# One kernel, new order: every step's rank set anew, and the first MLP's last outputs sorted by inner halves

## The chip, the cores and the metric

The kernel runs on one core of a Trainium2 chip. The metric is the device time of one execution in microseconds (us). The engines are TensorE (PE; its weight loads are listed as PEld), VectorE (DVE), ScalarE (ACT), GpSimd (POOL) and SyncE (SP), which issues the DMAs.

## The reference

An attention with exponential features, then two MLPs of two dense layers each:

```python
proj = q @ w_phi; proj -= max|proj|; q_p = [exp(proj), exp(-proj)]     # the same for k
kv = sum_s k_p[s]^T v[s];  z = sum_s k_p[s]
attn = (q_p @ kv) / (q_p . z + 1e-6)          # 4 batches, 8 heads, 576 tokens, 64 columns
x = attn as 2304 tokens x 512
h = x @ w1_in (512 x 2048);  g = elu(h);                    x = g @ w1_out (2048 x 512)
h = x @ w2_in (512 x 2048);  g = h * clip(h + 3, 0, 6) / 6; out = g @ w2_out
```

The weights come as float64 words and are turned into float32 pairs on the chip.

## The kernel before

**Attention.** Eight units (`unit(u)`), each two heads of two batches. A unit projects keys and queries (`PJ`, PE, L319), takes the largest magnitude (`MX`, DVE, L329), subtracts it (`SB`, DVE, L343), exponentiates keys (`EX`, ACT, L352), adds up `KV` on PE (L381), copies the sums out (`ST`, ACT, L390), transposes the queries (`QT`, PE, L395 and L401), exponentiates them (`QE`, ACT, L408), multiplies (`NM`, PE, L431), divides (`RT`, `RB`, DVE), transposes back (`XT`, PE, L453) and writes a piece of x (`XC`, ACT, L457).

**MLPs.** x has four token blocks of 512 and one of 256 (number 4), and four column chunks `d` of 128, of which chunks 0 and 1 are the one half of the inner dimension, 2 and 3 the other; in each half, the chunk is named by `kk` (chunks 0 and 2 are `kk` 0, chunks 1 and 3 are `kk` 1). Blocks 0 and 1 form pair 0, blocks 2 and 3 form pair 1. For each pair the first product is done by seven products (Winograd's form of Strassen's scheme, `P1` to `P7`, L711) instead of eight, block 4 directly (`H`, L725). Each operand is kept as a high and a low float32r part, and a product is three matmuls per piece. The operands are prepared by `prepare(m, pr)`: for each `kk` four sums or differences of x pieces (DVE, L688; called S1 to S4) and seven operands, each with a high part copied by ACT (L694) and a low part found by DVE or POOL (L697). x is overwritten in place. The hidden results pass through joins (DVE, L738), the activation (ACT, L745 to L748), the gate (DVE, L752), and a split into high (ACT, L756) and low (DVE, L759) in buffers `ga` (blocks 0 and 2) and `gb` (blocks 1, 3 and 4), two of each. The second product (`O`, PE, L776) makes four outputs (`d` 0 to 3) for each block, in the ring `y` of three PSUM banks; each output is added into x by DVE (`sums`, L788). That goes on for `NP` = 8 groups `g` of 256 hidden columns in each MLP: g 0 to 7 are the first, 8 to 15 the second. Weight conversion goes over ACT, DVE and POOL (L627 to L678).

**Order.** PE's order in the MLPs is written out by hand in the list `order`: products, outputs of this group and outputs left from the group before. In the last group of the first MLP (g = 7) the outputs of blocks 0 and 1 stand between the products of pair 1, those of blocks 2 and 3 at the end; the two halves of block 4's outputs (`kept`) come after the first two products of g = 8. The second MLP's operands can only be prepared when the outputs that complete x are added.

Every other engine's order is made by a planner, `in_order`, before the program is written out: it simulates all steps with assumed durations and, on each engine, takes among the steps that could start within `WINDOW` (0.3 us) of the soonest the one with the lowest rank. The engines then run these fixed orders, each waiting for its own data. The planner holds DVE steps marked `port` and POOL steps apart from each other. The ranks are times: in attention the unit's number times `PERIOD`, less the length of what follows, plus an offset for the kind of step; for operands the time at which PE is due to need them less `PREP` (16 us for the first MLP, 22 us for the second); for sums of outputs and for gates the time at which their product is due to end.

```python
s.rank = u * PERIOD - tail[id(s)] + BIAS.get(s.kind, 0.0)     # attention
rank = need[m, pr, op] - PREP[m]                              # operand's high and low part
when = clock + us                                             # sums and gates
if d == KD - 1:          # the last MLP-1 output of a block: its pair's prepare(1, ...) is listed
```

Of the kernel before, what the change touches and what calls it, by code (L numbers as in the profile page):

```python
# [24 lines left out]
PERIOD, PROJ, TURN = 21.5, 0.22, 0.19  # L25
BIAS = {
# [3 lines left out]
}  # L30
# [3 lines left out]
PREP = (16.0, 22.0)  # L34

# [8 lines left out]
class Step:  # L44
    def __init__(self, engine, us, fn, after=(), rank=0.0, takes=(), uses=(), port=False, behind=(), rows=128):
        self.engine, self.us, self.fn, self.rank, self.port, self.rows = engine, us, fn, rank, port, rows
        self.after, self.behind, self.takes = list(after), list(behind), list(takes)
        for t in uses:
            t.users.append(self)
        self.start = self.end = None  # L50


LATENCY = {"PE": 0.25, "DVE": 0.11, "ACT": 0.14, "POOL": 0.12, "SP": 2.2, "NONE": 0.0}
WINDOW = 0.3


def in_order(steps, rings):
# [13 lines left out]
    def soonest(s):  # L71
        t = max([0.0] + [x.end + LATENCY[x.engine] for x in s.after] + [x.start for x in s.behind])
        extra = {}
        for k in s.takes:
            had = taken[k.ring]
            at = len(had) + extra.get(k.ring, 0) - rings[k.ring]
            extra[k.ring] = extra.get(k.ring, 0) + 1
            if at < 0:
                continue
            if at >= len(had):  # L80
                return None
            for x in had[at].users:
                if x.end is None:
                    return None
                t = max(t, x.end + LATENCY[x.engine])
        return t

    known = {}
    while len(out) < len(steps):
# [23 lines left out]
        if s.port or s.engine == "POOL":  # L113
            port = s.end
# [34 lines left out]
def attention_then_two_mlps(  # L149
# [107 lines left out]
    def unit(u):  # L257
# [247 lines left out]
        add("ST", "ACT", 0.75, stat, after=[f"KV{j}{h}" for j in ("k0", "k1", "x8") for h in range(2)],  # L505
# [29 lines left out]
        for s in reversed(mine):  # L535
            tail[id(s)] = s.us + tail.get(id(s), 0.0)
            for x in s.after:
                tail[id(x)] = max(tail.get(id(x), 0.0), tail[id(s)] + LATENCY[x.engine])
        for s in mine:
            s.rank = u * PERIOD - tail[id(s)] + BIAS.get(s.kind, 0.0)  # L540
# [269 lines left out]

    def on(engine, us, fn, rank, after):
# [3 lines left out]
    def split(m, pr, op, kk, at, deps, e_hi, e_lo):  # L815
# [3 lines left out]
        hi = on(e_hi, (0.05 + 0.55 * size, 0.1 + 0.56 * size), bind_(x_hi, e_hi, pr, op, kk, at), rank, deps + home)  # L819
        lo = on(e_lo, (0.1 + 0.6 * size, 0.1 + 1.3 * size), bind_(x_lo, e_lo, pr, op, kk, at), rank, [hi])  # L820
# [4 lines left out]
    def prepare(m, pr):  # L825
        b0, b1 = 2 * pr, 2 * pr + 1
        POOL = nc.gpsimd
        for kk in range(2):
# [3 lines left out]
            def add(op, out_, in0, in1, alu, deps):  # L832
                e = POOL if soon else V
                s = on(e, (0.7, 1.4), bind_(x_add, e, out_, in0, in1, alu), need[m, pr, op] - PREP[m] - 1, deps)
# [4 lines left out]
            def cut(op, at, deps, e):  # L839
                here = soon and op in EARLY  # L840
                return split(m, pr, op, kk, at, deps, POOL if here else nc.scalar, POOL if here else e)

            r11 = cut("A11", a11, final[a11], V)
            r12 = cut("A12", a12, final[a12], POOL)
            r22 = cut("A22", a22, final[a22], V)
# [4 lines left out]
            cut("S2", a11, [s2], V)  # L850
            cut("S3", a21, [s3], POOL)
            cut("S1", a22, [s1], V)
            cut("S4", a12, [s4], POOL)
# [7 lines left out]
    for g in range(2 * NP):  # L861
# [63 lines left out]
    for g in range(2 * NP):  # L925
        m, w = g // NP, 2 * (g % NP)
        lead = first[g] - W_IN_LEAD
# [28 lines left out]
        lead = first_o[g] - W_OUT_LEAD  # L956
# [10 lines left out]
    def finish(m, g, b, fi, after, ps_, ring, when):  # L967
        key = (g, b, fi)
        if ring:
# [31 lines left out]
    for x in order:  # L1001
# [53 lines left out]
        else:  # L1055
# [6 lines left out]
            when = clock + us  # L1062
# [90 lines left out]
```

## Time and profile before

| | us |
|---|---|
| median of 3 runs | 938.45 (938.14 to 939.03) |
| the profiled execution: its time | 938.99 |
| the profiled execution: its span | 937.2 |
| PE busy | 903.2 (96%) |
| DVE, ACT, POOL busy | 677.9, 567.3, 398.0 |

The span runs from the first to the last instruction in the trace; the time is 1.8 us longer. Busy times are sums over stages that differ: PE is nearly always busy in the MLPs and less so in attention and between the stages.

### The profile page before, as it was taken

What the parts mean: (1) busy time and instruction counts of PE and PEld (TensorE: products, weight loads), DVE (VectorE), ACT (ScalarE), POOL (GpSimd) and SP (SyncE); (2) the same over time, 40 slices, a digit from 0 to 9 for tenths busy, and PEclk for the clock granted to TensorE, in tenths of its full rate; (3) what the DMA queues carried; (4) which work ended last, traced back from release to release, by engine and by line L of the source; (5) the groups of instructions that cost most, each with busy time, mean ns of one, the idle gap of its engine ahead of it and who ended that gap; (6) DMA issues with size and microseconds to landing.
All of it is one profiled execution on the core that took longest, in us unless ns stands there. A gap on an engine that the chain in (4) does not pass through costs nothing.

```text
span 937.2 us, 17621 instructions
## 1 busy us (share of the span) xinstructions
PE 903.2 (96%) x6792; PEld 759.3 (81%) x6792; DVE 677.9 (72%) x1202; ACT 567.3 (61%) x1207; POOL 398.0 (42%) x570
## 2 busy tenths in 40 slices
PE   8999999899999999999999978999999999999998
PEld 7888888778888888888888856888888888888886
DVE  6888887854868686868677789577777676767565
ACT  5687676877656565656566646765555554545331
POOL 0238721353535353535352555655544444444200
PEclk9999999999999999999999999999999999999999
DMA  7534420001111111111111000121111111110013
GB/s 223 158 114 119 134 82 2 1 13 44 39 52 40 51 38 53 37 54 37 55 37 55 11 12 23 58 68 56 56 62 40 50 42 54 36 54 26 1 66 137
DMA packets 42531, 53.69 MB, mean 57 GB/s; under 512 B 21328, under 2 KB 21456, under 8 KB 42448
## 3 DMA queue, kind: packets, MB, share of 16 engines
q1 hardware_dynamic: 42448, 52.57, 18.0%
q8 instruction: 53, 0.87, 0.4%
q14 instruction: 30, 0.25, 0.1%
HBM read 47.84 MB, written 4.72 MB: 56 GB/s over the span
## 4 chain that ended last, share of the span: by engine, by line
PE 88%; DVE 7%; ACT 4%; issue 1%; POOL 0%; POOLq 0%; ACTq 0%
PE ps_a L776 26%; PE ps_p L711 25%; PE ps_t L776 13%; PE ps_t L711 6%; PE ps_p L725 4%; PE ps_a L381 4%; PE ps_t L431 4%; PE ps_p L319 3%; ACT e L408 2%; DVE x L688 2%; DVE x_S L697 1%; PE ps_t L453 1%; PE ps_t L725 1%; DVE x_A L697 1%; DVE x L788 1%
## 5 line engine op out<-in xcount | busy, mean ns | idle before, releaser
L711 PE MATMUL ps_p<-x_S,w_in 128*128 128x512 f32 x630 | 159.3, 392 | 4.3 <-ACT mb L733 2.1
L788 DVE TENSOR_TENSOR x<-ps_a,x 128x512 f32<-128x512 f32 (+1 forms) x177 | 116.3, 660 | 49.5 <-PE ps_a L776 47.9
L711 PEld LDWEIGHTS ps_p<-x_S,w_in 128*128 128x128 f32 x630 | 118.5, 189 | 30.4 <-ACT mb L733 2.7
L669 POOL TENSOR_TENSOR w_in<-w_bi,w_in 128x256 fp32r<-128x256 f32 x128 | 94.8, 758 | 88.7 <-ACT w_in L665 88.5
L711 PE MATMUL ps_p<-x_A,w_in 128*128 128x512 f32 x468 | 117.4, 391 | 2.0 <-DVE ga L759 2.0
L636 POOL TENSOR_SCALAR w_a<-w_a 128x256 f32<-128x256 f32 x128 | 54.4, 426 | 125.7 <-ACT w_a L631 120.5
L711 PEld LDWEIGHTS ps_p<-x_A,w_in 128*128 128x128 f32 x468 | 86.9, 188 | 20.1 <-DVE ga L759 2.6
L652 POOL TENSOR_TENSOR w_bi<-w_bi,w_a 128x256 int32<-128x256 int32 x64 | 48.1, 755 | 113.1 <-DVE w_a L648 113.1
L776 PE MATMUL ps_a<-gb,w_out 128*128 128x512 f32 (+1 forms) x384 | 82.8, 357 | 6.8 <-DVE x L788 4.0
L788 DVE TENSOR_TENSOR x<-ps_t,x 128x512 f32<-128x512 f32 (+1 forms) x89 | 58.9, 662 | 37.9 <-PE ps_t L776 37.3
L776 PE MATMUL ps_a<-w_out,gb 128*128 128x512 f32 x336 | 82.7, 389 | 0.0
L776 PEld LDWEIGHTS ps_a<-gb,w_out 128*128 128x128 f32 x384 | 65.6, 191 | 18.7 <-DVE x L788 4.6
L776 PEld LDWEIGHTS ps_a<-w_out,gb 128*128 128x128 f32 x336 | 63.1, 188 | 13.1
L678 POOL TENSOR_TENSOR w_out<-w_bo,w_out 128x256 fp32r<-128x256 f32 x64 | 48.1, 752 | 59.1 <-ACT w_out L674 58.5
L776 PE MATMUL ps_a<-ga,w_out 128*128 128x512 f32 x258 | 64.3, 391 | 0.5 <-DVE ga L759 0.5
L652 POOL TENSOR_TENSOR w_bo<-w_bo,w_a 128x256 int32<-128x256 int32 x64 | 49.0, 767 | 33.1 <-DVE w_a L648 33.1
L329 DVE TENSOR_REDUCE mx<-ps_p 128x4 f32<-128x512 f32 (+1 forms) x80 | 50.3, 629 | 16.3 <-PE ps_p L319 16.2
L776 PE MATMUL ps_a<-w_out,ga 128*128 128x512 f32 x240 | 59.1, 391 | 1.9 <-ACT x L786 1.5
L733 ACT COPY mb<-ps_p 128x512 f32<-128x512 f32 x54 | 31.8, 589 | 45.5 <-PE ps_p L711 45.4
L752 DVE SCALAR_TENSOR_TENSOR ps_p<-ma,ps_p 128x512 f32<-128x512 f32 x66 | 45.7, 692 | 15.5 <-ACT ma L748 9.4
L776 PEld LDWEIGHTS ps_a<-ga,w_out 128*128 128x128 f32 x258 | 47.7, 188 | 10.4 <-DVE ga L759 0.9
L631 ACT ACTIVATE w_a<-w 128x256 f32<-128x256 f32 x128 | 54.5, 426 | 2.1 <-POOL w_bi L652 2.1
(109 smaller groups left out, 1907.0 us busy)
## 6 DMA issues: line engine op xcount, KB each, us to landing
w<-in_moe_w_in_dram SPq DMA_DIRECT2D x64, 256.0 KB, 2.6
w<-in_moe_w_out_dram SPq DMA_DIRECT2D x64, 256.0 KB, 2.6
vb<-in_v_dram SPq DMA_DIRECT2D x16, 288.0 KB, 4.3
out_dram<-x SPq DMA_DIRECT2D x18, 256.0 KB, 2.0
raw_k<-in_k_dram SPq DMA_DIRECT2D x7, 576.0 KB, 3.8
raw_q<-in_q_dram SPq DMA_DIRECT2D x7, 576.0 KB, 4.5
raw_k<-in_k_dram SPq DMA_DIRECT2D x1, 320.0 KB, 5.2
raw_q<-in_q_dram SPq DMA_DIRECT2D x1, 320.0 KB, 5.6
```

The source lines that it names most:

```text
L329: V.tensor_reduce(out=mx[:, :n], in_=P[j, h], axis=AX.X, op=ALU.max, apply_absolute_value=True)
L381: nc.tensor.matmul(out=acc[bb][f0:f0 + 64, h, half], lhsT=kp[p, i, half, f0:f0 + 64], rhs=vb[u % 2][p, r, h], start=(done.count(bb) == 1 a ...
L631: nc.scalar.activation(out=st["a"], in_=s.bitcast(F32).rearrange("p (n t) -> p n t", t=2)[:, :, 1], func=AF.Abs)
L636: nc.gpsimd.tensor_scalar(out=st["a"], in0=st["a"], scalar1=W_MOST, scalar2=W_LEAST, op0=ALU.min, op1=ALU.max)
L652: nc.gpsimd.tensor_tensor(out=b_, in0=b_, in1=st["a"].bitcast(I32), op=ALU.add)
L669: nc.gpsimd.tensor_tensor(out=t[:, 1], in0=F[key], in1=t[:, 0].bitcast(F32), op=ALU.subtract)
L678: nc.gpsimd.tensor_tensor(out=t[:, 1], in0=F.pop((m, w, 1, c)), in1=t[:, 0].bitcast(F32), op=ALU.subtract)
L711: nc.tensor.matmul(out=PS[ps_], lhsT=t[:, a_, kk], rhs=X[pr, op][x_][kk], start=(opens and i == 0), stop=(i == 5), skip_group_check=True,)
L725: nc.tensor.matmul(out=PS[ps_][:, 256 * fi:256 * fi + 256], lhsT=t[:, a_, kk], rhs=XB["x"][x_][2 * half + kk], start=(i == 0), stop=(i == ...
L752: V.scalar_tensor_tensor(out=PS[ps_], in0=MAIN[key], scalar=s, in1=PS[ps_], op0=o0, op1=o1)
L776: nc.tensor.matmul(out=o, lhsT=a_, rhs=b_, start=(fi + j == 0), stop=(fi == 1 and j == 2))
L788: V.tensor_tensor(out=part, in0=ps, in1=part, op=ALU.add)
```

## The change

The amount of work is the same: no instruction is added or taken away, the engines of all steps stay (`LO_ON_POOL` lists the same operands that had POOL before). What changes is the order.

- The planner's offsets in attention are per step name, with new values (54 numbers for 14), and its durations and waits are set anew: the projection 0.228 us an item for 0.22, a change of tile shape on PE 0.15 for 0.19, `ST` 0.60 for 0.75, the wait after a PE step 0.18 for 0.25, and DVE and POOL steps may overlap by 0.05.
- Operands (`a`, `h`, `l`: sum, high and low part, for MLP, pair, operand and `kk`), gates (`g`), sums of outputs (`y`), and weights (`wi`, `wo`) in groups 0, 1, 6 to 10 and 15 get offsets of their own in `SHIFT`.
- In g = 7 the outputs of blocks 0 and 1 go in the order (block, chunk) 00, 02, 12, 10, 01, 03, 13, 11, so that the four chunks with `kk` 0 come first; blocks 2 and 3 the same way. PE's order is otherwise the same in the MLPs.

```diff
-PERIOD, PROJ, TURN = 21.5, 0.22, 0.19
+PERIOD, PROJ, TURN = 21.5, 0.228, 0.15
 BIAS = {
-    "LD": 59.1, "ST": 26.0, "QE": -9.4, "RB": -64.2, "PJ": -18.6,
-    "NM": -30.3, "KV": -20.7, "QT": 0.7, "MX": 97.5, "EX": -26.0,
-    "XT": -28.4, "RT": -15.7, "SB": 28.1, "XC": -55.2,
+    "EX": -566.0, "EXk00": -549.9, "EXk01": -564.2, "EXk10": -554.5, "EXx80": -575.9, "KV": -449.5,
+    "KVk00": -403.0, "KVk01": 464.2, "KVk10": -395.6, "KVk11": -483.3, "KVx80": -437.6,
...
+SHIFT = {
...
+    "g1.4": -4.0, "g15.1": 6.4, "g15.2": 1.6, "g15.3": 1.9, "g15.4": -3.9, "g6.0": -0.9,
+    "g6.1": 0.4, "g6.2": -19.8, "g6.3": 4.8, "g6.4": -7.6, "g7.0": -0.4, "g7.1": 4.7, "g7.2": 96.7,
+    "g7.3": 150.1, "g7.4": -0.9, "g8.0": -80.4, "g8.1": 3.4, "g8.2": -2.7, "g8.3": 2.2, "g8.4": 1.5,
...
+    "y6.0": -1.7, "y6.2": 0.5, "y6.3": 1.1, "y6.4": 2.4, "y7.0": 0.4, "y7.1": 5.6, "y7.2": -21.8,
+    "y7.4": -207.9, "y8.1": 110.7, "y8.2": 3.3, "y8.3": -18.2, "y8.4": 0.2, "y9.0": -41.3,
...
+LAG = {"PE": 0.18, "DVE": 0.10, "ACT": 0.12, "POOL": 0.12, "SP": 2.2, "NONE": 0.0}
 LATENCY = {"PE": 0.25, "DVE": 0.11, "ACT": 0.14, "POOL": 0.12, "SP": 2.2, "NONE": 0.0}
 WINDOW = 0.3
+PORT = 0.05
...
         if s.port or s.engine == "POOL":
-            port = s.end
+            port = s.end - PORT
...
-        add("ST", "ACT", 0.75, stat, after=[f"KV{j}{h}" for j in ("k0", "k1", "x8") for h in range(2)],
+        add("ST", "ACT", 0.60, stat, after=[f"KV{j}{h}" for j in ("k0", "k1", "x8") for h in range(2)],
...
-            s.rank = u * PERIOD - tail[id(s)] + BIAS.get(s.kind, 0.0)
+            s.rank = u * PERIOD - tail[id(s)] + BIAS.get(s.name, BIAS.get(s.kind, 0.0))
...
+    def late(*tags):
+        return sum(SHIFT.get(t, 0.0) for t in tags)
...
+        hi = on(e_hi, (0.05 + 0.55 * size, 0.1 + 0.56 * size), bind_(x_hi, e_hi, pr, op, kk, at),
+                rank + late(f"h{m}{pr}{op}", f"h{m}{pr}{op}{kk}"), deps + home)
+        lo = on(e_lo, (0.1 + 0.6 * size, 0.1 + 1.3 * size), bind_(x_lo, e_lo, pr, op, kk, at),
+                rank + late(f"l{m}{pr}{op}", f"l{m}{pr}{op}{kk}"), [hi])
...
         elif g == NP - 1:
             z = prev_o
+            o0, o1 = ([x[i] for i in (0, 2, 6, 4, 1, 3, 7, 5)] for x in (o0, o1))
...
-        lead = first[g] - W_IN_LEAD
+        lead = first[g] - W_IN_LEAD + late(f"wi{g}")
...
-        lead = first_o[g] - W_OUT_LEAD
+        lead = first_o[g] - W_OUT_LEAD + late(f"wo{g}")
...
+        when += late(f"g{g}.{b}")
...
-            when = clock + us
+            when = clock + us + late(f"y{g}.{b}")
```

## Rows read from the trace of the kernel before

**Rows 1.** Busy time by stretch: stretch, its length, each engine's busy time (instructions), clock, DMA.

```profile
0.00:5.00 5.00, 3.64 (x18) 3.31 (x18) 0.00 (x0) 1.28 (x1) 0.89 (x10) 1.00 0.50 139
5.00:158.43 153.43, 141.35 (x3119) 125.01 (x3119) 126.04 (x258) 107.60 (x255) 60.20 (x78) 1.00 0.42 122
89.50:108.55 19.05, 17.90 (x405) 15.90 (x405) 16.20 (x34) 13.85 (x35) 15.98 (x17) 1.00 0.45 123
158.43:205.19 46.76, 42.22 (x289) 34.24 (x289) 33.59 (x54) 36.95 (x76) 19.10 (x19) 1.00 0.00 1
205.19:533.00 327.81, 327.67 (x1585) 275.39 (x1584) 232.38 (x411) 211.11 (x438) 142.71 (x216) 1.00 0.14 44
583.00:933.00 350.00, 349.89 (x1618) 291.36 (x1616) 240.06 (x416) 181.69 (x383) 147.81 (x224) 1.00 0.16 53
933.00:937.20 4.20, 0.37 (x2) 0.00 (x0) 0.69 (x1) 0.00 (x0) 0.00 (x0) 1.00 0.33 125
```

**Rows 2.** PE's waits over the span: us in total, times, longest.

```profile
PE ps_t L431 <- ACT e L408: 5.1, 12, 0.6
PE ps_a L776 <- DVE x L788: 4.0, 2, 3.2
PE ps_a L776 <- DVE gb L759: 2.7, 1, 2.7
PE ps_p L711 <- DVE ga L759: 2.0, 1, 2.0
PE ps_a L776 <- ACT x L786: 1.5, 1, 1.5
```

**Rows 3.** Busy time by stretch between the MLPs, columns as in the first group.

```profile
517.38:530.00 12.62, 12.62 (x63) 10.69 (x62) 8.75 (x15) 9.40 (x19) 4.85 (x7) 1.00 0.06 21
530.00:535.00 5.00, 5.00 (x29) 4.35 (x29) 3.69 (x6) 3.82 (x9) 2.72 (x4) 1.00 0.00 0
535.00:555.00 20.00, 12.53 (x60) 9.48 (x59) 20.00 (x26) 8.86 (x18) 15.24 (x13) 1.00 0.04 14
555.00:583.00 28.00, 23.50 (x106) 18.84 (x107) 23.41 (x38) 17.78 (x37) 11.23 (x12) 0.94 0.04 10
555.00:558.50 3.50, 3.50 (x12) 3.02 (x13) 3.18 (x9) 2.11 (x6) 1.40 (x2) 0.52 0.00 0
```

**Rows 4.** PE in order of time: start, length, line, tiles, idle time before.

```profile
522.02 1.52 PE L776 MATMUL ps_a<-gb,w_out 128*128 128x512 f32 x6
528.89 1.55 PE L776 MATMUL ps_a<-ga,w_out 128*128 128x512 f32 x6
549.48 1.46 PE L776 MATMUL ps_a<-gb,w_out 128*128 128x256 f32 x10 [2.70 <-DVE gb L759]
554.87 1.58 PE L776 MATMUL ps_a<-gb,w_out 128*128 128x256 f32 x6 [3.21 <-DVE x L788]
```

**Rows 5.** DVE and POOL in order of time, the same columns.

```profile
548.75 0.68 DVE L759 TENSOR_TENSOR gb<-ps_p,gb 128x512 fp32r<-128x512 f32 x1
550.43 3.45 DVE L697 TENSOR_TENSOR x_A<-x,x_A 128x512 fp32r<-128x512 f32 x2
554.41 0.74 DVE L788 TENSOR_TENSOR x<-ps_a,x 128x256 f32<-128x256 f32 x2
550.32 3.02 POOL L697 TENSOR_TENSOR x_S<-x,x_S 128x512 fp32r<-128x512 f32 x2
```

**Rows 6.** Groups of instructions, 500 to 600 us: busy time, mean ns, idle before.

```profile
L688 DVE TENSOR_TENSOR x<-x 128x512 f32<-128x512 f32 x16 | 13.3, 831 | 0.0
L694 ACT CAST x_S<-x 128x512 fp32r<-128x512 f32 x16 | 9.9, 622 | 8.9 <-DVE x L688 8.9
L697 DVE TENSOR_TENSOR x_S<-x,x_S 128x512 fp32r<-128x512 f32 x8 | 9.4, 1181 | 0.0
L697 DVE TENSOR_TENSOR x_A<-x,x_A 128x512 fp32r<-128x512 f32 x8 | 7.6, 954 | 0.1
```

**Rows 7.** One tile's instructions, 530 to 560 us: ns shortest/median/longest.

```profile
L697 DVE TENSOR_TENSOR x_S<-x,x_S x4: 676/1305/1787, 535.7 to 547.0; 128x512 fp32r<-128x512 f32 x4
```

More of the change, by code (lines that the diff above doesn't have):

```diff
@@ L34 @@
 PREP = (16.0, 22.0)
+SHIFT = {
[46 rows of a table added]
+}
+LO_ON_POOL = {
+    (0, 0): "A12 S3 S4", (0, 1): "A12 S3 S4", (1, 0): "A12 S3 S4", (1, 1): "A12 S3 S4",
+}
 class Token:
@@ L50, in __init__ @@
         self.start = self.end = None
+        self.lag = LATENCY[engine]
+LAG = {"PE": 0.18, "DVE": 0.10, "ACT": 0.12, "POOL": 0.12, "SP": 2.2, "NONE": 0.0}
 LATENCY = {"PE": 0.25, "DVE": 0.11, "ACT": 0.14, "POOL": 0.12, "SP": 2.2, "NONE": 0.0}
 WINDOW = 0.3
+PORT = 0.05
 def in_order(steps, rings):
@@ L71, in soonest @@
     def soonest(s):
-        t = max([0.0] + [x.end + LATENCY[x.engine] for x in s.after] + [x.start for x in s.behind])
+        t = max([0.0] + [x.end + x.lag for x in s.after] + [x.start for x in s.behind])
         extra = {}
@@ L84, in soonest @@
                     return None
-                t = max(t, x.end + LATENCY[x.engine])
+                t = max(t, x.end + x.lag)
         return t
@@ L263, in add @@
             s = step(engine, us, fn, after=[S_[x] for x in after], **kw)
-            S_[name], s.kind = s, name[:2]
+            S_[name], s.kind, s.name, s.lag = s, name[:2], name, LAG[s.engine]
             if stage:
@@ L833, in add @@
                 e = POOL if soon else V
-                s = on(e, (0.7, 1.4), bind_(x_add, e, out_, in0, in1, alu), need[m, pr, op] - PREP[m] - 1, deps)
+                tag = f"a{m}{pr}" + {a22: "S1", a21: "S3", a11: "S2", a12: "S4"}[out_]
+                s = on(e, (0.7, 1.4), bind_(x_add, e, out_, in0, in1, alu), need[m, pr, op] - PREP[m] - 1 + late(tag, f"{tag}{kk}"), deps)
                 for at in {out_, in0, in1}:
@@ L837, in add, with cut @@
                 return s
-            def cut(op, at, deps, e):
+            def cut(op, at, deps):
                 here = soon and op in EARLY
[L841 to L845, printed above, removed]
+                e = POOL if here or op in LO_ON_POOL[m, pr].split() else V
+                return split(m, pr, op, kk, at, deps, POOL if here else nc.scalar, e)
+            r11 = cut("A11", a11, final[a11])
+            r12 = cut("A12", a12, final[a12])
+            r22 = cut("A22", a22, final[a22])
             s1 = add("S2", a22, a21, a22, ALU.add, r22 + final[a21])
@@ L849, in prepare @@
             s4 = add("S4", a12, a12, a11, ALU.subtract, r12 + [s2])
[L850 to L853, printed above, removed]
+            cut("S2", a11, [s2])
+            cut("S3", a21, [s3])
+            cut("S1", a22, [s1])
+            cut("S4", a12, [s4])
     def prepare4(m):
```

4 lines of the change are left out of this document (1 added, 3 removed), and 52 rows, old and new, of tables (BIAS, SHIFT).

## The prediction

> **What bounds the kernel now.** I began with busy time by stretch [rows 1]. The reader is to subtract PE's busy time from each stretch's length: PE is idle for 1.4 us at the start, 12.1 in attention (5.00 to 158.43), 4.5 in the first group of the first MLP (to 205.19), 0.1 in the rest of that MLP, 0.1 in the second MLP after 583, and 3.8 at the end. Between the MLPs, 533 to 583, the finer cut [rows 3] gives 20.00 + 28.00 - 12.53 - 23.50 = 12.0 (PE is full up to 535 by its second row). The sum is 34.0, which is the span of 937.2 less PE's 903.2. So PE bounds the kernel wherever it is fed, and an order can win only in attention, in the first group, and between the MLPs. The start (no data yet) and the end (the last sum and its store) stay.
>
> Next, who makes PE wait [rows 2]: in attention mostly the exponentials of the queries (5.1 us in 12 waits); between the MLPs sums of outputs, gates and copies (4.0, 2.7, 2.0, 1.5).
>
> Last, the place between the MLPs in order of time. From 535 to 555 DVE is busy for 20.00 of 20 us and PE for 12.53 [rows 3]. The largest two waits there are waits for place in a queue: the output at 549.48 waits 2.70 us for `gb`, and the one at 554.87 waits 3.21 us for a sum that frees a PSUM bank [rows 4]. The `gb` split ran at 548.75, and the sum at 554.41, behind two low parts of operands that took 3.45 us from 550.43 [rows 5]. Those operands are wanted by PE many products later; their rank (due time less 22 us) put them ahead. After that wait the granted clock is 0.52 over the 3.50 us from 555 [rows 3], so at 1.2 GHz in nearly all of it: 0.48 x 3.50 = 1.7 us more.
>
> **The change part by part.** No instruction is added or removed, so the sum is made of idle time taken away or put in. It is made against the profiled execution's 938.99 us (span 937.2 and 1.8 around it); the median of the runs, 938.45, is 0.5 lower.
>
> *Between the MLPs (new output order, new offsets).* Count both engines from 535 to 583. DVE is busy for 20.00 + 23.41 = 43.4 us. PE is busy for 36.0 us, 34.3 at the full clock; what is lost is 48 - 34.3 = 13.7. If DVE goes on being the bound, PE loses DVE's work less 34.3.
>
> The new output order allows an inner half of pair 0 to be prepared earlier: its four outputs stand in the places of the first four, not up to the seventh. On DVE that is four sums and four low parts, eight instructions; one low part ran early before, so seven move. At 0.68 us (the shortest in [rows 7]) that is 4.8 us. The cover: DVE is idle for 12.62 - 8.75 = 3.9 us from 517.38 to 530 and for 1.3 to 535 [rows 3], 5.2 in all. ACT must copy high parts first, 0.62 us each [rows 6]: six need 3.7 of its 3.2 + 1.2 = 4.4 us idle there, so it just fits. If that cover is gone, all 4.8 us stay where they were.
>
> DVE's operand work is also stretched by POOL. The two low parts of 3.45 us stand beside POOL's 3.02 us from 550.32 [rows 5], and end 0.54 after it, about as if they had to wait for it. Over 500 to 600 the means of the three groups on DVE are 831, 1181 and 954 ns against 676 at the shortest [rows 6, 7]: 16 x 0.155 + 8 x 0.505 + 8 x 0.278 = 8.7 us of waiting.
>
> That makes three cases: half moved and stretching as before, 43.4 - 4.8 - 34.3 = 4.3 us still lost, a gain of 9.4; nothing moved, 9.1 lost, a gain of 4.6; moved and half of the stretching avoided, nothing lost, a gain of 13.7. Even the second needs the urgent steps to go first. The diff does that in one visible place: `y7.4`, the offset of just the sums that PE waited 3.21 us for, is -207.9, ahead of anything. I take the first case, **-9.4**, since planned order can move steps, but the planner knew of the stretching before and it was there all the same. Bounds: 0 (if the queues only change places) and -13.7.
>
> The new output order holds `ga` longer: the last output of block 0 moves from the fourth place to the sixth, which starts at 522.02 and ends 1.4 us later, at 523.4 [rows 4]. Block 2's two gated results then need a copy (0.6) and a split (0.7) each, two engines in turn, about 2.5 us: 525.9, and the output that reads them starts at 528.89 [rows 4]. It costs nothing by 3.0 us; that cover is PE's own products, and if DVE's moved work delays the splits by more, each further us is PE's.
>
> One wait isn't told to the planner: inner half 1 of pair 0 is listed when output (1, 3) comes, and (1, 1), which it also reads, now comes after it. Its first sum needs a copy and a low part of (1, 3) first, 0.62 + 0.68 us [rows 6, 7]; (1, 1) ends a product (some 1.4 us) later. Price nothing.
>
> *First group of the first MLP.* 4.5 us lost [rows 1], with DVE busy for 33.59 of 46.76: a matter of order, not throughput. Offsets for its operands, gates and weights (`h0`, `l0`, `g0`, `wi0`) could take all; I take **-1.0**. Bounds: -4.5, and +2 (a wait like the 2.0 of [rows 2] put in).
>
> *Attention.* 12.1 us lost. A typical unit (four of the eight are alike to 0.01 us in idle time) has 17.90 us of PE in 19.05, with DVE at 16.20 [rows 1]. Of 1.15 us idle, most is the wait for `QE`, where ACT does the `ST` copies and then four exponentials before `NM` can go. Offsets by name can put other PE work there, and durations nearer to the trace let the planner see the hole. But PE has little else ready at that place, or the hole would differ from unit to unit. I take **-2.0** of the 5.1 [rows 2]. Bounds: -9 (8 x 1.15), and +15, below.
>
> *The rest of the MLPs.* PE loses 0.1 + 0.1 us in 678 [rows 1], so offsets in groups 6, 9, 10 and 15 can only lose. I take **+0.5**; the bound is one wait of 3.2 us [rows 2].
>
> Sum: -9.4 - 1.0 - 2.0 + 0.5 = -11.9, so 938.99 - 11.9 = 927.1 for an execution like the profiled one and 926.6 for one like the median; I say **927.0**.
>
> **A rule against it.** What stretches DVE was read above from the rows: an operand's sum or low part ends only after POOL's instruction beside it. The Trainium skill's page "SBUF — State Buffer", section "SBUF: two separate sides", says that VectorE instructions with two SBUF inputs and GpSimd's share a pair of ports by an exclusive lock, held for the whole instruction, so the loser stops altogether. The trace agrees, with the 0.54 us. By this rule the moved work can be blocked in its new place too, where POOL is busy for 4.85 + 2.72 us [rows 3]. If all of that blocked, 4.8 + 7.6 us would have to go into 5.2 idle ones, and nothing would be gained by moving: the second rival.
>
> **The rivals.**
> 1. *More*: POOL and DVE are set apart (-13.7) and half of attention's idle goes (-6), the first group -2: 917.3, say 919. For it: all of it is idle time with no work missing. Against: DVE has 43.4 us to do in 48, and attention's holes are alike in each unit. Chance 0.10.
> 2. *The moved half is blocked or comes late*, other parts cancel: 938.99 - 4.6 + 0.5 = 934.9 (933 to 936.5). For it: POOL's 7.6 us and ACT with only 0.7 us to spare. Against: POOL's work there, weights, can shift too. Chance 0.15.
> 3. *No difference*: `ga` or DVE's queue gives back between the MLPs what the sums gain: 938. For it: DVE is full for 20 us. Against: two waits of 5.9 us are for steps which were ready in the queue. Chance 0.06.
> 4. *Slower, by attention alone*: the planner now counts 0.18 us after a PE step for 0.25 and lets DVE and POOL overlap; each engine's order is fixed, so a step that comes late on the chip holds all behind it. It decides if a unit's idle grows by 11.9 / 8 = 1.5 us, from 1.15 to 2.65, over eight units; at 3.1 it is 8 x 1.95 = 15.6, so 938.99 - 9.9 + 15.6 = 944.7. For it: DVE has 2.85 us to spare in a unit [rows 1], and more preparation of the first MLP moved into attention would use it. Against: `ST` and the projection were set to fit better, and no engine is full. Chance 0.14.
>
> **How the numbers follow.** My forecast, 922 to 932, has 0.55, the rivals 0.10, 0.15, 0.06 and 0.14. About 0.2%, 1.9 us, is what a measurement of this kernel can tell from no change. Faster: 0.55 + 0.10 + 0.15 = 0.80; the same 0.06; slower 0.14. The range takes in rival 1's 919 and rivals 2 and 3, 918 to 938; outside are the fourth (0.14) and an even better case (0.05).
>
> **What would show it.** Right: in the stretch between the MLPs, PE's idle falls from 12.0 to about 4, its waits for `gb` and for the sums of block 4 go, the clock stays at full there, and DVE has less idle between 517 and 533. A unit of attention is 18.8 us for 19.05. Rival 2 shows as low parts of 1.2 us or longer before 535; rival 3 as a wait for `ga` at the ninth output; rival 4 as units over 20.5 us. The prediction is wrong if PE waits between 205 and 533, or after 600, for more than 1 us in all, or if attention gains or loses more than the time between the MLPs.

## The result

The changed kernel takes 914.94 us (median of 4, 914.14 to 917.24) against 938.74 for the kernel before, a ratio of 0.9749 with a 95% interval from 0.9729 to 0.9769. The gain is 23.8 us where 11.5 was forecast, and the time lies below the stated range.

The profiled execution has a span of 911.8 us, 25.4 less. Busy time by stretch, columns as in [rows 1], with the stretches cut at the same places of the program: attention to the first MLP product; one typical unit of attention; the first group up to the first block-4 product of group 1; groups 1 to 7 up to the block-4 product of group 7; the stretch between the MLPs up to the second half of the block-4 product of group 9; the rest.

```profile
5.00:150.57 145.57, 138.86 (x3114) 125.05 (x3114) 124.87 (x253) 108.00 (x253) 58.99 (x76) 0.99 0.44 127
106.02:124.08 18.06, 17.71 (x405) 15.91 (x404) 15.58 (x34) 13.34 (x31) 2.81 (x6) 1.00 0.36 98
150.57:192.28 41.71, 41.47 (x295) 35.05 (x292) 32.16 (x56) 36.40 (x75) 15.23 (x13) 1.00 0.03 8
192.28:513.77 321.49, 321.43 (x1551) 270.73 (x1549) 226.92 (x408) 209.97 (x436) 149.07 (x222) 1.00 0.14 45
513.77:573.52 59.75, 57.38 (x283) 48.51 (x282) 51.98 (x89) 44.22 (x92) 39.82 (x46) 0.97 0.11 36
573.52:907.50 333.98, 333.89 (x1542) 278.28 (x1541) 226.96 (x397) 169.87 (x353) 133.81 (x205) 1.00 0.16 51
518.00:522.00 4.00, 3.82 (x15) 3.30 (x16) 4.00 (x8) 3.11 (x7) 2.37 (x2) 0.60 0.00 0
```

PE's idle time in attention is now 6.7 us (12.1 in [rows 1]), in the first group 0.2 (4.5), between the MLPs 2.4 (12.0 in [rows 3]). The typical unit has 0.35 us idle for 1.15. All of PE's waits above 0.3 us in the changed kernel:

```profile
PE ps_t L459 <- DVE shq L407: 2.9, 2, 2.6
PE ps_a L840 <- ACT ga L820: 2.1, 1, 2.1
PE ps_t L495 <- ACT x L521: 1.8, 5, 0.3
PE ps_t L495 <- ACT e L472: 1.4, 3, 0.7
PE ps_t L303 <- POOL ident masks.py:199: 1.4, 1, 1.4
PE ps_p L383 <- DVE shk L407: 0.4, 1, 0.4
```

Against [rows 2]: the wait for the queries' exponentials fell from 5.1 to 1.4 us, though 1.8 us of waits for copies of x (`XC`) came in at the same products. Those for sums of outputs (4.0) and for `gb` (2.7) are gone. Two waits are new: 2.1 us for `ga`, and 2.6 us in the first unit, where a transpose of queries now stands ahead of projections and PE waits for its input `shq`.

To see where the 25.4 us come from, both traces are cut at the same matmuls. The first column runs from the second unit's first projection (18.7 us before, 19.8 after), since the start before it differs between executions of one plan by up to 2 us (last section). PE's first matmuls of the five places start at 18.70, 158.19, 205.03, 527.46 and 598.67 us before, and at 19.77, 150.57, 192.29, 513.77 and 573.52 after.

| | attention from unit 2 | first group | groups 1 to 7 | between the MLPs | rest |
|---|---|---|---|---|---|
| before | 139.49 | 46.84 | 322.43 | 71.21 | 338.54 |
| after | 130.81 | 41.72 | 321.47 | 59.75 | 338.24 |
| gain | 8.7 | 5.1 | 1.0 | 11.5 | 0.3 |

Runs below that share the plan of a stage show how far one profile can be trusted: between the MLPs and in the first group they agree to 0.1 us (between the MLPs 66.4 to 66.5 in four runs, 59.8 in three), but in attention they differ by up to 2 us (133.1 and 131.2 in e11_start_shift and e21_start_shift_halves, which are alike there).

### The profile page after: what moved, and what is told of

It reads as the page before. It is cut to its first block, busy times and chain, and to the rows that moved or that the text cites. A ratio compares the mean times of both kernels' runs of the same rounds, so it can differ in the third digit from the quotient of the medians.

```text
span 911.8 us, 17612 instructions
## 1 busy us (share of the span) xinstructions
PE 897.1 (98%) x6792; PEld 760.9 (83%) x6792; DVE 663.6 (73%) x1202; ACT 569.7 (62%) x1207; POOL 397.8 (44%) x570
## 3 DMA queue, kind: packets, MB, share of 16 engines
q1 hardware_dynamic: 42448, 52.57, 18.7%
## 4 chain that ended last, share of the span: by engine, by line
PE 96%; ACT 2%; DVE 2%; issue 0%; POOL 0%; POOLq 0%; DVEq 0%
PE ps_a L840 29%; PE ps_p L775 27%; PE ps_t L840 14%; PE ps_t L775 6%; PE ps_t L495 4%; PE ps_p L789 4%; PE ps_p L383 4%; PE ps_a L445 4%; PE ps_t L789 1%; PE ps_t L459 1%; PE ps_t L517 1%; ACT e L472 1%; DVE mx L393 0%; PE ps_t L303 0%; ACT x L521 0%; DVE shq L407 0%
## 5 line engine op out<-in xcount | busy, mean ns | idle before, releaser
L775 PE MATMUL ps_p<-x_S,w_in 128*128 128x512 f32 x630 | 157.1, 389 | 0.0
L775 PEld LDWEIGHTS ps_p<-x_A,w_in 128*128 128x128 f32 x468 | 87.1, 188 | 18.1 <-DVE ga L823 0.5
L840 PEld LDWEIGHTS ps_a<-gb,w_out 128*128 128x128 f32 x384 | 65.2, 189 | 10.8
```

The lines of the kernel that those rows point to most:

```text
L775: nc.tensor.matmul(out=PS[ps_], lhsT=t[:, a_, kk], rhs=X[pr, op][x_][kk], start=(opens and i == 0), stop=(i == 5), skip_group_check=True,)
L840: nc.tensor.matmul(out=o, lhsT=a_, rhs=b_, start=(fi + j == 0), stop=(fi == 1 and j == 2))
```

## What a unit of attention looks like now

PE in order of time in a typical unit of the kernel before, up to its second set of products (columns as in [rows 4]):

```profile
91.41 3.65 PE L381 MATMUL ps_a<-vb,kp 128*64 128x65 f32 x128
94.99 1.09 PE L395 MATMUL ps_t<-ident,shq 128*128 128x128 f32 x8
96.82 0.66 PE L395 MATMUL ps_t<-ident,shq 128*128 128x128 f32 x4
97.80 1.62 PE L431 MATMUL ps_t<-st,e 128*64 128x65 f32 x48 [0.32 <-ACT e L408]
103.49 3.02 PE L431 MATMUL ps_t<-st,e 128*64 128x65 f32 x96 [0.60 <-ACT e L408]
```

The same place in the changed kernel:

```profile
108.01 1.15 PE L445 MATMUL ps_a<-vb,kp 128*64 128x65 f32 x32
109.47 0.60 PE L459 MATMUL ps_t<-ident,shq 128*128 128x128 f32 x4
110.00 1.15 PE L445 MATMUL ps_a<-vb,kp 128*64 128x65 f32 x32
111.09 0.66 PE L459 MATMUL ps_t<-ident,shq 128*128 128x128 f32 x4
112.32 0.66 PE L459 MATMUL ps_t<-ident,shq 128*128 128x128 f32 x4
112.92 1.62 PE L495 MATMUL ps_t<-st,e 128*64 128x65 f32 x48
118.16 3.02 PE L495 MATMUL ps_t<-st,e 128*64 128x65 f32 x96 [0.35 <-ACT x L521]
```

And ACT before (first fence) and after (second fence), the copies of the sums (`st`) and the queries' exponentials (`e`):

```profile
95.11 0.66 ACT L390 COPY st<-ps_a 128x260 f32<-128x260 f32 x2 [2.61 <-PE ps_a L381]
95.68 3.05 ACT L408 ACTIVATE e<-ps_t 128x512 f32<-128x512 f32 x6
```

```profile
110.11 1.09 ACT L472 ACTIVATE e<-ps_t 128x512 f32<-128x512 f32 x2
111.20 0.65 ACT L454 COPY st<-ps_a 128x260 f32<-128x260 f32 x2
111.78 2.32 ACT L472 ACTIVATE e<-ps_t 128x512 f32<-128x512 f32 x4
```

Before, PE did 128 of a unit's 160 key products at a stretch and only then the transposes. ACT stood idle for 2.61 us, then had copies and exponentials for 3.6 us in one piece, and PE waited for them at 97.80 (0.32 us) and again for the next ones at 103.49 (0.60 us). Now 96 of a unit's key products are done before this place, the rest comes in two pieces of 32, and transposes stand between them: ACT has its first exponentials before the copies, and the products find theirs ready at 112.92.

Which part of the change does this can be read from unit lengths, taken from one unit's query projection to the next one's:

| run | parts (letters as in the experiments) | 2 to 3 | 3 to 4 | 4 to 5 | 5 to 6 | 6 to 7 | 7 to 8 |
|---|---|---|---|---|---|---|---|
| before | none | 18.37 | 19.06 | 19.05 | 19.05 | 20.13 | 20.18 |
| e18_old_attention_port | P S O B | 18.12 | 19.06 | 19.05 | 19.05 | 19.06 | 19.05 |
| e3_attention_alone | P A L | 17.97 | 18.38 | 18.13 | 19.59 | 20.85 | 21.05 |
| after | all | 17.97 | 18.38 | 18.12 | 18.11 | 18.06 | 18.05 |

With attention's old offsets and lags, a typical unit keeps its 19.05 us whatever else changes; with the new ones it has some 18.1. That is not GpSimd's work leaving the unit: it is busy for 16.53 us in the unit from 89.38 in e18_old_attention_port (19.05 us) and for 15.99 in the unit from 87.91 in the changed kernel (18.11). The last units need the offsets of the first MLP's start (S) too: without them they are 20 to 21 us long.

## Between the MLPs now

The new wait, in order of time on PE, and the steps that it hangs on, on DVE and ACT:

```profile
515.20 0.86 PE L840 MATMUL ps_a<-ga,w_out 128*128 128x512 f32 x3
518.18 1.52 PE L840 MATMUL ps_a<-ga,w_out 128*128 128x512 f32 x3 [2.12 <-ACT ga L820]
```

```profile
504.78 1.42 DVE L752 TENSOR_TENSOR x<-x 128x512 f32<-128x512 f32 x2
507.91 1.19 DVE L761 TENSOR_TENSOR x_A<-x,x_A 128x512 fp32r<-128x512 f32 x1
514.57 0.69 DVE L816 SCALAR_TENSOR_TENSOR ps_p<-ma,ps_p 128x512 f32<-128x512 f32 x1
515.89 1.10 DVE L752 TENSOR_TENSOR x<-x 128x512 f32<-128x512 f32 x1
```

```profile
509.16 0.63 ACT L810 ACTIVATE ma<-ma 128x512 f32<-128x512 f32 x1
517.02 0.62 ACT L758 CAST x_S<-x 128x512 fp32r<-128x512 f32 x1 [1.09 <-DVE x L752]
517.55 0.58 ACT L820 CAST ga<-ps_p 128x512 fp32r<-128x512 f32 x1
```

Four operand sums (L752, from 504.78) and four low parts (L761, from 499.62) of the second MLP now run on DVE before the first block-4 product at 513.77; in the kernel before, two low parts and no sum ran ahead of that place. The activation of block 2's second result ended at 509.8. Its gate ran on DVE at 514.57, behind sums of outputs, a join, a split and two operand steps. Its copy ran on ACT only at 517.55, behind the copy of an operand at 517.02, for which ACT itself stood idle 1.09 us until a sum on DVE (515.89) was done. PE waits 2.12 us, and the granted clock is 0.60 over the 4 us from 518, which costs 0.40 x 4 = 1.6 us.

DVE's operand work, 474.9 to 574.9 us, columns as in [rows 6]:

```profile
L752 DVE TENSOR_TENSOR x<-x 128x512 f32<-128x512 f32 x16 | 11.9, 751 | 0.1
L761 DVE TENSOR_TENSOR x_A<-x,x_A 128x512 fp32r<-128x512 f32 x8 | 7.0, 880 | 0.0
L761 DVE TENSOR_TENSOR x_S<-x,x_S 128x512 fp32r<-128x512 f32 x8 | 5.6, 708 | 0.0
```

Against the shortest of 676 ns [rows 7] the stretching beside POOL's work is 16 x 0.075 + 8 x 0.204 + 8 x 0.032 = 3.1 us, where it was 8.7.

## The experiments

The parts of the change are: (P) DVE and POOL steps may overlap by 0.05 us in the planner; (A) attention's offsets by step name; (L) attention's durations and lags; (S) offsets of the first MLP's start; (O) the order of the last outputs; (B) the other offsets, nearly all between the MLPs. All runs at a glance; the stage columns are lengths as in the table above, each from one profiled execution. Times are compared by the ratio: the kernel before, run beside each group of experiments, took 938.5 to 938.9 us, and 940.4 beside e13_g72, e16_kinds_all and e21_start_shift_halves.

| run | parts | ratio to before (95%) | attention from unit 2 | first group | between |
|---|---|---|---|---|---|
| before | none | 1 | 139.5 | 46.8 | 71.2 |
| e14_port_alone | P | 0.9957 (0.9940 to 0.9974) | 140.4 | 46.2 | 66.4 |
| e17_port_010 | P at 0.10 | 0.9979 (0.9970 to 0.9988) | 140.1 | 46.2 | 68.7 |
| e1_halves_alone | O | 0.9964 (0.9951 to 0.9977) | 139.5 | 46.8 | 68.3 |
| e3_attention_alone | P A L | 0.9972 (0.9959 to 0.9985) | 138.1 | 51.3 | 66.4 |
| e10_no_shift | P A L O | 0.9950 (0.9933 to 0.9967) | 139.1 | 50.8 | 63.4 |
| e20_start_old_attention | P S | 0.9879 (0.9864 to 0.9894) | 137.4 | 42.8 | 66.4 |
| e19_start_old_lags | P A S | 0.9905 (0.9890 to 0.9920) | 139.6 | 43.3 | 66.5 |
| e11_start_shift | P A L S | 0.9794 (0.9774 to 0.9814) | 133.1 | 41.7 | 63.9 |
| e21_start_shift_halves | P A L S O | 0.9764 (0.9738 to 0.9790) | 131.2 | 41.7 | 63.4 |
| e2_no_halves | P A L S B | 0.9889 (0.9871 to 0.9907) | 131.0 | 41.7 | 73.6 |
| e4_old_attention | S O B | 1.0038 (1.0023 to 1.0053) | 138.0 | 49.2 | 74.7 |
| e18_old_attention_port | P S O B | 0.9808 (0.9792 to 0.9825) | 137.7 | 42.8 | 59.8 |
| e16_kinds_all | all, A by kind only | 0.9915 (0.9895 to 0.9934) | 140.5 | 51.2 | 59.8 |
| e8_gates_in_time | all, two gates' offsets 0 | 0.9754 (0.9739 to 0.9768) | 131.4 | 41.7 | 63.0 |
| e13_g72 | all, one gate's offset 0 | 0.9795 (0.9767 to 0.9823) | 132.0 | 41.7 | 65.7 |
| after | all | 0.9749 (0.9729 to 0.9769) | 130.8 | 41.7 | 59.8 |

### The order of outputs alone, and taken away

To the kernel before (e1_halves_alone); the second run takes the same line out of the changed kernel (e2_no_halves).

```diff
+            o0, o1 = ([x[i] for i in (0, 2, 6, 4, 1, 3, 7, 5)] for x in (o0, o1))
```

> The kernel before with only the new order of the last outputs of the first MLP; all ranks, lags and durations are old. Theory of the prediction: preparing one inner half earlier moves 4.8 us of VectorE work into its idle time before 535, so the time falls by about 4.8 us, to some 934. Rival: ranks decide, because the sums and gates that PE waits for still stand behind operands; then the time stays within 2 us of before, and a wait for ga may come in at the first output of blocks 2 and 3.

Measured: 936.41 us, 2.5 less than before, all of it between the MLPs (71.2 to 68.3). That lies between the two expectations: half of what the moved work was priced at. The wait for `gb` is gone and one of 2.7 us for a sum is left, but a wait for `ga` at a product of the second MLP grew from 2.0 to 4.2 us.

> The changed kernel with the old order of the outputs; all new offsets stay. Theory of the prediction: it loses the 4.8 us of moved VectorE work, so about 919.7. Rival one: ranks alone do it, so it is within 2 us of 914.9. Rival two: the offsets were set for the new order and do harm without it, so all 11.5 us between the MLPs go, 926 or more.

Measured: 928.06 us; the second rival. The stretch between the MLPs is 73.6 us, worse than before. PE in order of time, its two long waits there:

```profile
527.05 3.36 PE L840 MATMUL ps_t<-gb,w_out 128*128 128x512 f32 x6 [6.47 <-ACT gb L820]
565.82 3.38 PE L840 MATMUL ps_t<-w_out,gb 128*128 128x512 f32 x6 [4.14 <-ACT gb L820]
```

The first is for the results of block 3. Their gates ran on DVE at 515.70 and 516.29, but their copies on ACT only at 525.29 and 526.42, behind copies of operands; the offset `g7.3`, +150.1, holds for all steps of such a result. What holds up the second, a group later, was not followed. After such a wait six matmuls take 3.36 us for 1.52, with a granted clock of 0.50. So part B fits the new order and does harm in the old one.

### Attention's part alone, and with the new order

```diff
 SHIFT = {
-    "a00S11": 0.3, "a00S2": 20.2, "a00S20": 16.6, "a00S21": 9.2, "a00S3": 35.0, "a00S30": -13.0,
...
 }
...
-            o0, o1 = ([x[i] for i in (0, 2, 6, 4, 1, 3, 7, 5)] for x in (o0, o1))
```

The changed kernel with an empty `SHIFT` and the old order (e3_attention_alone), and with an empty `SHIFT` alone (e10_no_shift).

> The kernel before with only the new offsets by step name in attention and the new durations and lags of the planner; no offset in the MLPs, old order of outputs. Theory A: attention's units are shortened by these alone, 1 us in each of six and 2 in the last two, and the first group of the MLP keeps its 4.5 us of waits: a gain of 8 to 10, some 929 to 931. Theory B: the units could only be shortened because the offsets of the first MLP's weights and operands took their VectorE and GpSimd work away: a gain of 2 to 4 (the prediction took 2).

Measured: 935.73 us, a gain of 3.2, so theory B by the size. The stages say more. The seventh unit's projections begin 92.9 us after the second's, where it was 96.4 before; the last two units give back 2.1 of the 3.5, and the first group is 4.5 us longer, since the first MLP's operands come late (PE waits 3.9 us at once for `x_S` there). And 4.8 us came between the MLPs, where no offset is new.

> The changed kernel without any offset in the MLPs: attention's offsets and lags new, outputs in the new order. If gains add, its gain is that of the attention part plus that of the order alone. If order and offsets need each other between the MLPs, it stays about 8 to 11 us above the changed kernel, some 923 to 926; if the order alone carries that stretch, some 915 to 919.

Measured: 934.75 us, a gain of 4.2 where the two parts' gains add to 5.7: roughly the first expectation. The 923 to 926 and 915 to 919 were far off, since attention's part fails in the first group as in the run before it. Between the MLPs it gains 7.9 us, about the sum of the 4.8 and 2.9 of the two parts.

### One constant

```diff
+PORT = 0.05
...
-            port = s.end
+            port = s.end - PORT
```

To the kernel before (e14_port_alone), and the same with 0.10 (e17_port_010).

> The kernel before with one constant changed: VectorE and GpSimd steps may overlap by 0.05 us in the planner. The stretch between the MLPs gained 4.8 us in the run with attention's offsets alone, and this constant is the only part of that kernel that reaches the MLPs directly. Theory A: the constant does it, 933 to 935. Theory B: it came from where VectorE and GpSimd stand when the MLPs begin, an accident of the order; then within 2 us of before.

Measured: 934.70 us; theory A. A constant to which the prediction gave no price makes 4.1 us. PE in order of time at the place of [rows 4]:

```profile
543.91 1.60 PE L783 MATMUL ps_a<-gb,w_out 128*128 128x256 f32 x12
545.34 0.88 PE L783 MATMUL ps_t<-gb,w_out 128*128 128x256 f32 x6
547.10 0.97 PE L783 MATMUL ps_a<-gb,w_out 128*128 128x256 f32 x6 [0.88 <-DVE x L795]
```

The wait of 2.70 us for `gb` is gone, and that of 3.21 us for the sum is 0.88, without the offset `y7.4` in which the prediction saw the remedy.

> The kernel before with the planner's allowed overlap of VectorE and GpSimd steps at 0.10 us in place of 0 (0.05 alone gave 934.7). Theory A, the overlap is a truer picture of the chip, so 0.10 gives about as much or more: 933 to 936. Theory B, a small shift only tips choices among steps that could start within 0.3 us, and where they fall is chance: then the gain is of another size or sign, outside 933 to 936.

Measured: 936.64 us; theory B. Twice the overlap gives half the gain: the first waits stay away, but PE waits once for 7.6 us for `ga`. So the constant does not help in proportion. That a small shift tips choices among steps that could start within 0.3 us of each other fits this, but the planner's choices were not followed one by one.

### The start of the first MLP

```diff
 SHIFT = {
-    "a10S11": -5.6, "a10S2": -23.3, "a10S21": 8.9, "a10S3": -44.7, "a10S31": -1.5, "a10S4": -16.2,
...
-    "y7.4": -207.9, "y8.1": 110.7, "y8.2": 3.3, "y8.3": -18.2, "y8.4": 0.2, "y9.0": -41.3,
...
 }
```

Of the offsets in the MLPs only those for operands of the first MLP, groups 0 and 1, and weights of groups 0 to 2 stay, with the old order: with all of attention's part (e11_start_shift), with its old durations and lags (e19_start_old_lags), and with all of attention old (e20_start_old_attention). The last two keep the overlap of 0.05.

> The kernel before with attention's new offsets and lags and, in the MLPs, only the offsets that bear on the start of the first MLP (its operands, gates and sums of groups 0 and 1, weights of groups 0 to 2); old order of outputs, nothing new between the MLPs. Theory A, attention and the start need each other: the first product begins some 7 us earlier and group 0 ends some 12 earlier than before, where attention's offsets alone had them 0.3 earlier and 4 later; with the 4 to 5 us that the stretch between the MLPs gained in that run, 921 to 923. Theory B, the offsets of the start do little: as with attention's offsets alone, 934 to 936.

Measured: 919.69 us; theory A, and 1.3 us better than it. The first group ends 10.1 us earlier than before.

> Attention's old offsets, durations and lags, the offsets of the first MLP's start, overlap 0.05, nothing else (with attention's new offsets and lags: 919.7; with the overlap alone: 934.7). Theory A: attention and the start need each other, so the units stay at 19.05 us and the start gains at most 2: 932 to 936. Theory B: the start's offsets alone take the 4.5 us of waits in the first group: 928 to 931.

Measured: 927.78 us; theory B, slightly better. The start's offsets alone take 4.0 us in the first group and 2.1 in the attention ahead of it.

> Attention's new offsets and the offsets of the first MLP's start, overlap 0.05, but the planner's old durations and lags in attention (with the new ones: 919.7). Theory A: the offsets do the work and the lags little, 918 to 922. Theory B: the new offsets were found with the new lags, and with the old ones the units lose their order: 926 or more.

Measured: 930.37 us; theory B. With the old lags the new offsets by name are no better than the old ones (930.4 against 927.8): from the second unit, attention takes 139.6 us instead of 133.1. The new durations and lags with the old offsets were not run, so what the lags do by themselves is open.

### Attention taken away

```diff
 BIAS = {
-    "EX": -566.0, "EXk00": -549.9, "EXk01": -564.2, "EXk10": -554.5, "EXx80": -575.9, "KV": -449.5,
...
+    "LD": 59.1, "ST": 26.0, "QE": -9.4, "RB": -64.2, "PJ": -18.6,
...
-LAG = {"PE": 0.18, "DVE": 0.10, "ACT": 0.12, "POOL": 0.12, "SP": 2.2, "NONE": 0.0}
+LAG = {"PE": 0.25, "DVE": 0.11, "ACT": 0.14, "POOL": 0.12, "SP": 2.2, "NONE": 0.0}
...
-PORT = 0.05
+PORT = 0.0
```

To the changed kernel, with the old durations too (e4_old_attention); the second run keeps the overlap (e18_old_attention_port).

> The changed kernel with attention's old offsets, durations, lags and no overlap of VectorE and GpSimd steps; all offsets in the MLPs and the new order stay. Theory A: the start gains little without attention's offsets (a unit keeps its 19.05 us), so only the stretch between the MLPs gains, 926 to 929. Theory B: it is the first MLP's preparation leaving attention alone that shortens the units; then 918 to 921.

Measured: 942.38 us, slower than before, which neither theory had. Attention (138.0) is not what is slow; the first group is 2.4 us longer than before, and between the MLPs it needs 74.7 us, and all of PE's larger waits there are for gated results:

```profile
PE ps_a L830 <- DVE gb L813: 4.3, 1, 4.3
PE ps_t L830 <- ACT gb L810: 3.9, 1, 3.9
PE ps_a L830 <- ACT gb L810: 2.4, 1, 2.4
PE ps_a L830 <- DVE ga L813: 1.3, 1, 1.3
```

> The changed kernel with attention's old offsets, durations and lags, but with the overlap of 0.05 (without it this gave 942.4). Theory A: the offsets between the MLPs need only the overlap that they were set with, so that stretch gains its 11.5 us and the start little: 925 to 928. Theory B: those offsets fit one plan as a whole, and another attention ahead of them spoils them: 935 or more.

Measured: 921.34 us. Between the MLPs it is the changed kernel to 0.04 us (59.79 and 59.75), so theory A holds there, and the total is 4 us better than theory A because the start's offsets gain 4.0 us in the first group and 1.8 in attention even so. The constant of 0.05 alone is worth 21 us in this plan, and 4.1 in the plan before; with the new attention it was not taken away by itself.

### Offsets by name

```diff
-BIAS = {
...
-    "KVx81": -447.7, "LD": 59.1, "MX": 2429.2, "MXk00": -583.1, "MXk01": -1129.2, "MXk10": 2368.2,
-    "MXk11": -298.5, "MXq00": -147.0, "MXq01": -234.7, "MXq10": -37.9, "MXq11": -7.1,
...
+BIAS = {'EX': -566.0, 'KV': -449.5, 'LD': 59.1, 'MX': 2429.2, 'NM': 182.6, 'PJ': -480.4, 'QE': 377.8, 'QT': 675.8, 'RB': -1590.3, 'RT': -402.3, 'SB': -741.7, 'ST': -61.4, 'XC': -1557.2, 'XT': 438.5}
```

The new table has 71 numbers, 14 by kind and 57 by step name (not 54 in all with forty by name). A value by kind holds only for steps without one by name.

> The changed kernel with attention's offsets by kind of step only: the fourteen new values for kinds stay, the forty by step name go; lags and all else as in the changed kernel. Theory A: the order between steps of a kind, above all key products set against each other and query transposes brought between them, is what shortens a unit, so its 18.1 us go back to 19 and the time to 920 to 926. Theory B: the lags and the kinds do it, within 2 us of 914.9.

Measured: 932.15 us, further than theory A said. The stretch between the MLPs is as in the changed kernel (59.81); attention and the first group are 19 us longer. PE's waits for the queries' exponentials are 6.5 us in 9, the longest 2.2, and for the back transposes 3.2 us in 6. The units are 18.3 to 20.8 us long.

This does not show that the order inside a kind is what shortens a unit. For nine of the fourteen kinds (`MX`, `KV`, `NM`, `QE`, `QT`, `RB`, `RT`, `XC`, `XT`) every step has a value by name in the changed kernel, so the value by kind orders nothing there. In this run it comes into force: all maxima get 2429.2, where they had -1129.2 to 2368.2. The run thus shifts whole kinds against each other as well, and the two effects are not told apart.

### The wait for `ga` that is left

```diff
-    "g6.1": 0.4, "g6.2": -19.8, "g6.3": 4.8, "g6.4": -7.6, "g7.0": -0.4, "g7.1": 4.7, "g7.2": 96.7,
-    "g7.3": 150.1, "g7.4": -0.9, "g8.0": -80.4, "g8.1": 3.4, "g8.2": -2.7, "g8.3": 2.2, "g8.4": 1.5,
+    "g6.1": 0.4, "g6.2": -19.8, "g6.3": 4.8, "g6.4": -7.6, "g7.0": -0.4, "g7.1": 4.7, "g7.2": 0.0,
+    "g7.3": 0.0, "g7.4": -0.9, "g8.0": -80.4, "g8.1": 3.4, "g8.2": -2.7, "g8.3": 2.2, "g8.4": 1.5,
```

Both (e8_gates_in_time), and `g7.2` alone (e13_g72).

> The changed kernel with two offsets set to 0: those that put the gates of blocks 2 and 3 of the last group 97 and 150 us back (rank only). In the changed kernel PE waits 2.1 us for such a gate, and the granted clock is 0.60 for 4 us behind it, 1.6 us more. Theory A: the gate stood behind operands in VectorE's queue because of its rank, so the wait and the slow clock go: 911 to 912. Theory B: the gates put in front push operands back, and PE waits for those: 914 to 918.

Measured: 915.76 us, ratio 0.9754 against the changed kernel's 0.9749; theory B. The wait for `ga` is gone, and PE waits 3.1 us for an operand instead:

```profile
PE ps_p L775 <- DVE x_S L761: 3.1, 1, 3.1
```

> The changed kernel with the offset of the gates of block 2 of the last group at 0 instead of 96.7; that of block 3 stays at 150.1 (both at 0: 915.8, with a wait of 3.1 us for an operand in place of the 2.1 for ga). Theory A: only block 2's gates are urgent, so the wait for ga and the slow clock go and no operand is late: 911 to 912.5. Theory B: whatever goes ahead of operands in a full VectorE queue makes one late: 914 to 917.

Measured: 920.27 us, worse than theory B. The wait moves to the next gated results (`gb`), and to the weights of the second product:

```profile
PE ps_a L840 <- ACT gb L820: 3.8, 1, 3.8
PE ps_a L840 <- ACT w_out L738: 1.6, 1, 1.6
PE ps_a L840 <- POOL w_out L742: 1.5, 1, 1.5
```

So neither of these two ranks alone wins the time of the wait for `ga`: in both runs something else came late. Other ways, such as moving the operand copy that ACT waited on, were not tried.

### The fourth corner

The edit is that of e11_start_shift, with the new order kept.

> Fourth corner between the MLPs: attention and the start as in the changed kernel, the new order of outputs, but no offset between the MLPs (neither: 919.7; offsets alone: 928.1; both: 914.9). Theory A: the order moves 4.8 us of VectorE work forward by itself, since operands' old ranks already put them ahead; 915 to 917, and the offsets give the rest. Theory B: the order alone only makes ga late, as its buffers are held longer; 919 or more, and only both together gain.

Measured: 916.71 us, ratio 0.9764 (0.9738 to 0.9790). By the stages, from one profile each, between the MLPs: neither 63.9, order alone 63.4, offsets alone 73.6, both 59.8. The order by itself is worth 0.5 us there, far from theory A's 3 to 5; the offsets by themselves cost 9.7; together they gain 4.1. Theory B's price is not right either: the wait for `ga` is 1.4 us, 2.2 without the order. What it says of both together is. The whole time does lie in theory A's range, but 2 us of its gain are in attention, where the two plans are alike, and the intervals of the two runs overlap; so the stages decide. e11_start_shift, without O and B, already has 19 of the 23.8 us. No run was faster than the changed kernel.

## Why the prediction was wrong

**What bounds the kernel: right.** PE idle by stage was the gain that could be had, and each stage gained nearly all of its bound: attention 8.7 from the second unit (bound 9), the first group 5.1 (bound 4.5), between the MLPs 11.5 (bound 13.7). The first group could exceed its bound because PE's busy time fell too, there from 42.3 to 41.5 us and in all by 6.1, with the same instructions. Why is not shown. It is not the slow clock, of which the changed kernel has more (1.6 us between the MLPs and 0.44 x 3.50 = 1.5 in the first unit, for 1.7 before), and busy time fell by 0.9 even in groups 1 to 7, where neither trace has a wait.

**The step that failed: attention, -2.0, and the first group, -1.0.** 3.0 us were taken where 13.8 came. Against the profiled span the sum was short by 25.4 - 11.9 = 13.5 us; 10.8 of it is here, 2.1 between the MLPs and 1.8 in the rest, less 1.1 that the changed kernel's first unit started late. The reason given, that PE has little else ready at the place of the hole, or the hole would differ from unit to unit, was wrong. The changed kernel's rows show, with the same work, transposes between pieces of the key products, ACT fed earlier, and 0.35 us idle in a unit for 1.15. So a hole that is alike in each unit was a sign of an order that is alike in each. That attention's offsets and lags together do this is shown by e18_old_attention_port against the changed kernel: all else new, a typical unit stays at 19.05 us. How it divides between the two is open: the new offsets with the old lags lose (e19_start_old_lags), the other half was not run, and e16_kinds_all changes more than the order inside a kind. The bounds had the right size; the choice of a fifth of the bound had no row behind it.

**The start was tied to attention, which the sum did not have.** The two terms were costed apart. e3_attention_alone shows that attention's part alone gains 1.4 us there and gives back 4.5 in the first group (51.3 us for 46.8); e20_start_old_attention that the start alone gets 6.1 us in both; together, in e11_start_shift, 6.4 + 5.1 = 11.5.

**Between the MLPs, -9.4: right in place, too small by 2.1.** Of the three cases it is between the first and the third: operand work moved ahead, as the DVE rows from 504.78 show, and of the stretching 5.6 of 8.7 us went, where the prediction left all of it. But moving was not what mattered most: by e14_port_alone 4.8 us come from a constant, with neither the order nor an offset, and by e1_halves_alone and e21_start_shift_halves the order alone gives 2.9 or 0.5 us, not 4.8. The remedy that the prediction named, `y7.4`, was not needed for the two waits. It was not tried by itself. That the term came within 2.1 us is thus in part luck. The clock did not stay full there, as the prediction's signs had it.

**`ga` held longer, priced at nothing with 3.0 us of cover: wrong.** The cover counted copies and splits alone. The gate before them stood 4.8 us in DVE's queue (its input ended at 509.8, it ran at 514.57) and the copy behind it another 2.3 us in ACT's, and the 2.1 us wait came at the ninth output, as rival 3 said it would show. With the clock it costs 3.7 us. It does not decide the time, and e8_gates_in_time shows that setting these two ranks to 0 buys nothing.

**The rest of the MLPs, +0.5: wrong sign, small.** Groups 1 to 7 are 1.0 us shorter and the end 0.3, with no wait in groups 1 to 7 of either trace to account for it. By the runs, some 0.35 us go with S (322.07 in e11_start_shift for 322.43) and 0.6 with B (321.48 in e18_old_attention_port). How they shorten it is open.

**The rivals.** The first, nearest with its 919, had a chance of 0.10, and asked for half of attention's idle; it was more. The even better case, which came, had 0.05, and that stands outside the five chances, which already add up to 1.00. Rival 2 did not come: low parts of 1.05 and 1.19 us before 513 show that some of the work ahead was still stretched, but two thirds of the stretching went. The fourth, slower by attention alone, did not come, but units of the length that it named do: 20.85 and 21.05 us in e3_attention_alone, where the first MLP's offsets are missing. The prediction's own sign of being wrong, attention gaining more than the time between the MLPs, was not met (8.7 for 11.5), though it was attention, with the first group, that the sum missed.

## What to carry to other kernels

When the work is fixed and one engine's idle time is the whole loss, an order that is set anew as a whole can take most of it, as here: count the bound of each stage as possible, and ask for a row before taking less. A hole that repeats in each round can be a sign of the order, not of missing work; look whether the engine that feeds it stood idle just before. Some offsets fit one plan alone: without attention's part this change lost 6 us, without the new output order 13, and without attention's part and the constant of 0.05 us 27. Others hardly matter: without part B it lost 2. So such a change is tested whole first, and its parts in pairs.

## What was not expected of the hardware

In the changed kernel PE was full from 478 to 516, waited once for 2.12 us, and the granted clock was then 0.60 over the 4 us from 518, so at 1.2 GHz in most of it; that cost 1.6 us more. In the kernel before it fell after waits of 2.70 and 3.21 us within 6 us.

A wait of this length did not always do that. In the first unit PE waits 2.58 us for `shq` in the changed kernel and in e8_gates_in_time, whose attention has the same plan. The stretch behind it, 10.50 to 14.00, in the changed kernel (first line) and in e8_gates_in_time (second line):

```profile
10.50:14.00 3.50, 3.50 (x30) 3.17 (x32) 2.13 (x4) 2.12 (x4) 0.00 (x0) 0.56 1.05 344
10.50:14.00 3.50, 3.35 (x76) 3.06 (x76) 3.40 (x6) 2.90 (x6) 0.00 (x0) 1.00 1.01 339
```

The same wait was followed by a clock of 0.56 in one execution and of 1.00 in the other. With a first projection that took 2.00 us for 1.19, this puts the second unit's first projection at 19.77 us in the changed kernel and at 17.60 in e8_gates_in_time. Stage lengths from one profile are therefore taken from there on. A single wait of two to three microseconds cost 1.5 and 1.6 us more in two places, and nothing in a third.
